# Second layers of tiles 1 and 2 as one 2x2 block problem of seven products

## The chip, the cores and the metric

One Trainium2 chip, one core. The metric is device time in microseconds. TensorE (PE) does the matmuls, VectorE (DVE), ScalarE (ACT) and GpSimd (POOL) the elementwise work, SyncE (SP) issues every DMA of the kernel from one queue.

## The reference

Causal attention over 4 batches, 12 heads, 448 positions and head size 64, then a two-layer network on its output:

```
scores = scale * q @ k^T, masked above the diagonal; attn = softmax(scores); o = attn @ v
x = o with its heads side by side                  # 1792 tokens x 768
h = x @ w_in                                        # 1792 x 2048
g = where(h > 0, h, exp(min(h, 0)) - 1)
out = g @ w_out                                     # 1792 x 768, float32
```

The weights w_in (768 x 2048) and w_out (2048 x 768) come as 64-bit floats; q, k and v as 32-bit floats.

## The kernel before

The 448 positions are cut into four chunks of 112. A *tile* (g = 0 to 3 in the code, tiles 1 to 4 here) is one chunk of all four batches: 448 token columns. Everything is kept transposed, so that a tile of x is 6 blocks of 128 rows by 448 columns, a tile of the hidden layer 16 such blocks, a tile of the output 6.

Attention works on pairs of heads (6 pairs p, 4 batches b, so 24 units a tile). For each unit TensorE makes scores, VectorE adds the mask and finds the largest (L326), ScalarE takes the exponential with its sum (L330), one of three engines scales (L564 to L570), TensorE transposes (L539), ScalarE or VectorE copies the transposes (L543, L544), TensorE multiplies by v into the accumulator `av` (L518). Tile g needs g + 1 chunks of k and v. In tiles 3 and 4 the scores are made from q and k split into a high and a low part (`parts`, L429), three matmuls each.

A product of the network is accurate to float32 by splitting both factors into a high and a low part in a short format and adding three matmuls (`three`, L679: high by high, high by low, low by high). Only the first 8 of 16 row blocks of tile 1's first layer use one plain float32 matmul (L703). `hi_lo` (L647) makes the split: a copy on ScalarE (or VectorE), a subtraction on VectorE (or GpSimd).

A weight piece is read as 64-bit words, converted to float32 by five steps (L620 on VectorE, L624 on ScalarE, L625 on VectorE, L628 on ScalarE, L631 on GpSimd) and stored to DRAM (`kin`, `kout`) for the tiles that follow. This is `weights` (L599). Pieces of w_in are 768 elements wide per partition (16 pieces), pieces of w_out 512 (24 pieces: 6 row blocks e, 4 groups x of 4 hidden blocks).

Tiles 1 and 2 go through the network one after the other: first layer (`emit_h`, 16 x 6 blocks), then second layer (`emit_o`, 6 x 16 blocks). `emit_h` ends a hidden block with the activation on ScalarE (L710, L711) and VectorE (L712) and splits it at once into gh and gl (L715, L716). While tile 2 uses the weights, `mixed` (L661) also makes four sums or differences of quarter blocks of each layer's weights and stores them (`sin`, `sout`).

Tiles 3 and 4 are taken together, as a 2x2 block problem: the weight halves by output rows and by inner dimension, and the two tiles as two column blocks. A product scheme with seven block products in place of eight (GROUPS, L810: 1, 2, 6, 7, 4, 5, 3) needs sums of weights (`sin`, `sout`, read back by `raw_piece`), differences of activations (`halves`, L788) and sums of results (`results`, L814). `mixed_h` does the first layer so, `mixed_o` the second. Their x rows (`xs`) wait in SBUF from attention on.

Buffers are rings: `PLACES` (L273) gives their number. A `Ring` hands its places out in a fixed order; a `Heap` hands out the place that was released first. Rows of 448 columns share one pool of SBUF, eight PSUM banks are shared by `hp` (3), `p` (4) and `av` (1).

The order of work is written by a planner (`Plan`). Every step is listed with estimated costs, what it reads and writes and, for matmuls, a due time; due times go back from a step to those it needs. It starts, step by step, the work that can start first, of several the one due first, and where two engines could do a step, the first unless the other would end sooner. What it finds is the fixed order of instructions of each engine. `SPREAD` (L983) says where attention is listed among the network's blocks, in estimated microseconds of network matmuls: tile 2's attention from 0 to 125, tile 3's to 185, tile 4's to 240. Tile 1's first layer is 67 of these, its second 60, tile 2's layers 60 each. `plan.cap` bounds the due time of `mixed` to 8 (LATER) after the block it is listed with.

## Time and profile before

| what | value |
|---|---|
| median of 3 runs | 644.68 us (644.46 to 646.44) |
| the profiled execution | 645.02 us, span 643.2 us |
| TensorE matmul busy | 620.4 us, 96%, 4032 instructions |
| VectorE, ScalarE, GpSimd busy | 517.0, 441.4, 192.4 us |
| granted clock, mean | 0.995 |
| DMA | 124.25 MB, 193 GB/s over the span |

A busy share is an average over stages. Matmuls are pipelined and overlap, so their busy time is more than their number times the distance between two starts. In the lists by group the figures behind the bar are busy time, the mean duration in ns, and how long the engine stood idle just before, with what ended that.

### The profile page before, as it was taken

To read this page: it belongs to the slowest core of one execution; us is meant where nothing else is said; L and a number is where in the kernel's file an instruction comes from. 1 tells how busy PE (TensorE), PEld (TensorE's weight loads), DVE (VectorE), ACT (ScalarE), POOL (GpSimd) and SP (SyncE) were. 2 spreads that over 40 slices of the span, in tenths; PEclk is the share of its full clock that TensorE was granted. 3 is DMA by queue.
4 is the path that set the end of the run, shared out by engine and by line. 5 is a ranking of instruction groups with operands and counts; after the bars stand their busy time and mean duration, and the time that the engine had idled before them with its cause. 6 is when DMAs were issued, how large, how long until landed. Compare 5 with 4: busy or idle time off the path is not lost. (4 is left out here: it accounts for less than half of the span.)

```text
span 643.2 us, 11841 instructions
## 1 busy us (share of the span) xinstructions
PE 620.4 (96%) x4032; PEld 523.9 (81%) x4032; DVE 517.0 (80%) x1192; ACT 441.4 (69%) x1007; POOL 192.4 (30%) x166
## 2 busy tenths in 40 slices
PE   5799998999999999999999999999999999999997
PEld 4655586888886888888888887899999988999996
DVE  5875888898766997999787898998767899998611
ACT  6898888885766988878786768666544867463300
POOL 1352434334243445453332323210100462100000
PEclk9999997999999999999999999999999999999999
DMA  9998576779887577586748765576343233353121
GB/s 229 300 369 319 197 242 211 231 237 319 276 259 236 171 252 237 171 265 221 243 153 247 217 195 166 182 236 193 115 107 115 98 100 98 121 144 104 44 61 44
DMA packets 108124, 124.25 MB, mean 193 GB/s; under 512 B 39840, under 2 KB 87968, under 8 KB 108064
## 3 DMA queue, kind: packets, MB, share of 16 engines
q1 hardware_dynamic: 108064, 123.50, 61.8%
q8 instruction: 32, 0.52, 0.3%
q14 instruction: 28, 0.23, 0.1%
HBM read 92.80 MB, written 30.67 MB: 192 GB/s over the span
## 5 line engine op out<-in xcount | busy, mean ns | idle before, releaser
L653 DVE TENSOR_TENSOR whl<-w,whl 128x768 fp32r<-128x768 f32 (+1 forms) x114 | 108.1, 952 | 17.8 <-ACT whl L650 16.3
L330 ACT ACTIVATE a<-a,nm 112x112 f32<-112x112 f32 (+3 forms) x192 | 97.0, 519 | 34.6 <-DVE nm L326 34.5
L650 ACT ACTIVATE whl<-w 128x768 fp32r<-128x768 f32 (+1 forms) x90 | 69.3, 772 | 52.1 <-PE op L684 27.0
L326 DVE CUSTOM_DVE_ANT_0 a<-sc,mask 112x112 f32<-112x112 f32 (+3 forms) x192 | 74.7, 442 | 26.2 <-PE sc L488 12.1
L631 POOL TENSOR_TENSOR w<-w,w 128x512 int32<-128x512 int32 (+1 forms) x40 | 62.7, 1569 | 98.3 <-DVE w L625 70.8
L682 PE MATMUL op<-gh,whl 128*128 128x448 f32 x192 | 73.3, 382 | 1.5 <-ACT whl L650 1.4
L684 PE MATMUL op<-gh,whl 128*128 128x448 f32 x192 | 70.9, 369 | 1.3 <-DVE whl L653 1.2
L683 PE MATMUL op<-gl,whl 128*128 128x448 f32 x192 | 70.1, 365 | 0.0
L682 PE MATMUL hp<-ph,whl 128*128 128x448 f32 x168 | 61.9, 369 | 1.7 <-DVE u L777 1.7
L682 PE MATMUL op<-ph,whl 128*128 128x448 f32 x168 | 61.5, 366 | 0.0
L684 PE MATMUL op<-ph,whl 128*128 128x448 f32 x168 | 61.5, 366 | 0.0
L683 PE MATMUL op<-pl,whl 128*128 128x448 f32 x168 | 61.5, 366 | 0.0
L683 PE MATMUL hp<-pl,whl 128*128 128x448 f32 x168 | 61.5, 366 | 0.0
L684 PE MATMUL hp<-ph,whl 128*128 128x448 f32 x168 | 61.4, 366 | 0.0
L682 PE MATMUL hp<-xh,whl 128*128 128x448 f32 x144 | 57.1, 396 | 3.0 <-ACT whl L650 3.0
L684 PE MATMUL hp<-xh,whl 128*128 128x448 f32 x144 | 53.9, 374 | 0.2 <-DVE whl L653 0.2
L683 PE MATMUL hp<-xl,whl 128*128 128x448 f32 x144 | 53.6, 372 | 0.0
L518 PEld LDWEIGHTS av<-at,v 112*64 112x64 f32 x864 | 41.6, 137 | 12.0 <-issue 7.3
L518 PE MATMUL av<-at,v 112*64 112x112 f32 x864 | 49.4, 263 | 0.0
L539 PE MATMUL tr<-ident,a 112*112 112x112 f32 x432 | 48.9, 263 | 0.0
L658 POOL TENSOR_TENSOR w<-w 128x384 f32<-128x384 f32 (+1 forms) x29 | 27.1, 933 | 63.2 <-DVE w L658 29.4
L539 PEld LDWEIGHTS tr<-ident,a 112*112 112x112 f32 x432 | 41.5, 133 | 5.4 <-issue 0.4
(121 smaller groups left out, 1392.4 us busy)
## 6 DMA issues: line engine op xcount, KB each, us to landing
w<-in_w_in SPq DMA_DIRECT2D x16, 768.0 KB, 6.8
w<-in_w_out SPq DMA_DIRECT2D x24, 512.0 KB, 5.6
w<-kin SPq DMA_DIRECT2D x28, 384.0 KB, 4.2
k<-in_qk SPq DMA_DIRECT2D x30, 224.0 KB, 4.3
kin<-w SPq DMA_DIRECT2D x16, 384.0 KB, 3.0
kout<-w SPq DMA_DIRECT2D x24, 256.0 KB, 4.5
sin<-w SPq DMA_DIRECT2D x16, 384.0 KB, 3.3
w<-kout SPq DMA_DIRECT2D x24, 256.0 KB, 4.1
```

The costliest lines, as they stand in the source:

```text
L326: plan.add(dve(n, lambda: nc.vector.tensor_tensor_reduce(out=a()[:, c], in0=sc()[:, c], in1=mask[:, S - n:], op0=ALU.add, op1=ALU.min, sca ...
L330: plan.add(act(n, lambda: nc.scalar.activation(a()[:, c], a()[:, c], AF.Exp, bias=nm()[:, x:x + 1], scale=-1.0, accum_out=su()[:, x:x + 1] ...
L518: nc.tensor.matmul(av()[half_of(half), chunk(o["b"])], o["v"]()[:, half, i], at()[:, chunk(x)], start=i == 0, stop=i == g,)
L539: nc.tensor.transpose(tr()[:, chunk(x)], o["a"][half]()[:, chunk(i)], ident)
L631: plan.add(pool(size, lambda: nc.gpsimd.tensor_tensor(out=wf().bitcast(I32), in0=wf().bitcast(I32), in1=low().bitcast(I32), op=ALU.add)), ...
L650: act(n, lambda: nc.scalar.activation(h(), x(), AF.Copy)),
L653: sub = lambda eng: lambda: eng.tensor_tensor(out=l(), in0=x(), in1=f32(h()), op=ALU.subtract)
L658: two = lambda eng: lambda: eng.tensor_tensor(out=out(), in0=x(), in1=y(), op=op)
L682: nc.tensor.matmul(acc(), wh(k), xh(), start=first, stop=False, skip_group_check=more)
L683: nc.tensor.matmul(acc(), wh(k), xl(), start=False, stop=False, skip_group_check=more)
L684: nc.tensor.matmul(acc(), wl(k), xh(), start=False, stop=last, skip_group_check=more)
```

## The change

Tile 1's first layer is followed directly by tile 2's first layer. The 32 activated hidden blocks stay in SBUF as whole rows `G`; they are split later, product by product. The second layers of tiles 1 and 2 are then done together by `mixed_o(0)`, the same seven products as for tiles 3 and 4, with three accumulators from `hp`. Each of its 28 weight pieces is read back from DRAM and split.

For that, all of w_out is converted before: `pair_o` is listed twelve times between 62 and 122 on the scale of SPREAD, each time two pieces, and makes their sums into the buffer of the second piece's words. The sums of w_in are made by `pair_i`, eight times between 130 and 215, which reads two pieces again. Attention is listed at 0 to 64 (tile 2), 64 to 122 (tile 3) and 122 to 215 (tile 4). Tile 1's first layer is 67 on that scale, tile 2's 60, the seven products 104.

The x rows of tiles 3 and 4 are stored to `xdram` and read back when `mixed_h` begins its first two groups. Rows that lived in two rings (`x`, `g`) come from one heap of 53 places, and `w` and `w6` are heaps; `k` has three places where it had five, and for tile 2 a k place holds two batches. The split q and k of tile 3 lie in rows of the heap instead of `w6`. The planner's estimate of a DMA is 60 plus 0.3 for each byte of a row, at most 390 GB/s, where it was 260. Of kout only the parts that a product reads are stored. `convert`, `fetch` and `in_two` are the parts of `weights`, taken apart.

```diff
     PLACES = dict(
-        q=2, k=5, v=5, a=8, at=5, x=18, g=2 * FT, m=2, ob=2, w6=8, w=5, nm=4, su=4, rr=4, hp=3, p=4, av=1, row=SPARE,
+        q=2, k=3, v=5, a=8, at=5, m=2, ob=2, row=53, w6=8, w=5, nm=4, su=4, rr=4, hp=3, p=4, av=1, bank=0,
     )
-    ROWS = ("q", "k", "a", "at", "x", "g", "m", "ob", "row")
+    ROWS = ("q", "k", "a", "at", "m", "ob", "row")
...
+    xdram = dram.tile([2, NP, P, S], F32, name="xdram")
+    xkept = {}
...
     def split_x(g, p, av):
+        if g >= 2:
+            x = new("ob", [P, S], name="xs")
+            take(x, av)
+            k = xkept[g - 2, p] = Buf(None, lambda: xdram[g - 2, p])
+            dma(224, P, lambda: nc.sync.dma_start(out=k(), in_=x()), [x], [k])
+            return
         if g == 0:
-            x = xf[p] = new("g", [P, S], name="xf")
-            plan.add([
-                act(S, lambda: nc.scalar.activation(x(), av(), AF.Copy)),
-                dve(S, lambda: nc.vector.tensor_copy(x(), av())),
-            ], [av], [x])
-        if g >= 2:
-            x = xs[g, p] = new("x", [P, S], name="xs")
...
-            return
-        xh = new("x", [P, S], F32R, "xh")
-        xl = new("x", [P, S], F32R, "xl")
+            x = xf[p] = row("xf")
+            take(x, av)
+        xh, xl = row("xh", F32R), row("xl", F32R)
         plan.add(act(S, lambda: nc.scalar.activation(xh(), av(), AF.Copy)), [av], [xh])
         plan.add(
             dve(S, lambda: nc.vector.tensor_tensor(out=xl(), in0=av(), in1=f32(xh()), op=ALU.subtract)), [av, xh], [xl]
         )
         xt[g, p] = xh, xl
...
+        done(q0, k0)
...
+    def parts(g, x, n):
+
+        if g == SPLIT:
+            th, tl = new("row", [P, S], F32R, "kh"), new("row", [P, S], F32R, "kl")
+            hi, lo = (lambda: th()[:, :n]), (lambda: tl()[:, :n])
+            get = lambda d, i, c: (th, tl)[i]()[d, c]
+            h = th, tl
...
+        for b in range(0, B, 2) if g == 1 else ():
+            k, t = new("k", [P, S]), new("v", [CP, 2, 2, 2, D], name="v2")
+            src = qk[b:b + 2, 2 * p:2 * p + 2, :, 1, :n].rearrange("b h d c -> (h d) b c")
+            dma(n, 2 * P, lambda k=k, src=src: nc.sync.dma_start(
+                out=k().rearrange("p (b c) -> p b c", b=2), in_=src
+            ), [], [k])
+            for i in range(2):
+                dma(112, 2 * CP, lambda t=t, i=i, b=b: nc.sync.dma_start(out=t()[:, i], in_=v[b + i, p, :, :, :2]), [], [(t, i)])
+                ks.append((None, [k], lambda d, x, c, k=k, i=i: k()[d, i * n + c.start:i * n + c.stop]))
+                vs.append((t, lambda half, x, t=t, i=i: t()[:, i, half, x]))
...
+    def convert(key):
+        r, w = words.pop(key), new("w", [P, KT, P])
+        n = KT if key[0] == "i" else 4
...
+        if key[0] == "i":
+            done(r)
+            home, src = kin[key[1]], wf
         else:
-            by = (lambda t: t) if key[0] == "i" else lambda t: t.rearrange("p (h k) c -> p h k c", h=2)
...
+            h = key[1] // HALF_E
+            home = kout[key[1]].rearrange("p (h f) c -> p h f c", h=2)[:, h:, 2 * key[2]:2 * key[2] + 2]
+            src = lambda: wf().rearrange("p (h f) c -> p h f c", h=2)[:, h:]
+        k = kept[key] = Buf(None, lambda: home)
+        dma(n * 64, P, lambda: nc.sync.dma_start(out=home, in_=src()), [w], [k])
+        return w if key[0] == "i" else (w, r)
+
+    def fetch(f):
+        w, k = new("w", [P, KT, P]), kept["i", f]
+        dma(KT * 64, P, lambda: nc.sync.dma_start(out=w(), in_=k()), [k], [w])
+        return w
+
+    def in_two(w, n):
+        t = new("w6", [P, 2, KT, P], F32R, "whl")
+        hi_lo(lambda: t()[:, 0, :n], lambda: t()[:, 1, :n], lambda: w()[:, :n], n * P, (t, 0), (t, 1), w)
+        done(w)
+        return t, (lambda k: t()[:, 0, k]), (lambda k: t()[:, 1, k])
 
...
+        if layer == 1:
+            add(b(1), b(0), b(1), n, ALU.add, [(wb, 0)], [(wb, 1)])
+            add(b(0), a(0), b(0), n, ALU.subtract, [(wa, 0)], [(wb, 0)])
+            add(a(0), b(1), a(0), n, ALU.subtract, [(wb, 1)], [(wa, 0)])
+            add(a(1), a(1), a(0), n, ALU.subtract, [(wa, 0)], [(wa, 1)])
+            for i, w in enumerate((wa, wb)):
+                dma(2 * h * 64, 2 * P, lambda i=i, w=w: nc.sync.dma_start(
+                    out=sin[r][:, :, i], in_=w().rearrange("p (h k) c -> p h (k c)", h=2)
+                ), [w], [(k, i)])
+            return
+        m = lambda i: lambda: f32(into().rearrange("p k c w -> p (k c w)"))[:, i * n:i * n + n].rearrange("p (k c) -> p k c", k=h)
+        add(m(3), b(0), b(1), n, ALU.add, [wb], [(into, 3)])
+        add(m(1), a(0), b(0), n, ALU.subtract, [(wa, 0), (wb, 0)], [(into, 1)])
+        add(m(0), m(3), a(0), n, ALU.subtract, [(wa, 0), (into, 3)], [(into, 0)])
+        add(m(2), a(1), m(0), n, ALU.subtract, [(wa, 1), (into, 0)], [(into, 2)])
+        dma(4 * h * 64, 4 * P, lambda: nc.sync.dma_start(
+            out=sout[x, :, :, :, r].rearrange("p h i c -> p (h i) c"),
+            in_=f32(into().rearrange("p k c w -> p (k c w)"))[:, :4 * n].rearrange("p (m c) -> p m c", m=4),
+        ), [into], [k])
...
     def emit_h(g, f, k, due):
         if k == 0:
...
+            if g == 0:
+                for n in range(0 if f == 0 else f + EARLY, min(f + EARLY + 1, FT)):
+                    load64(("i", n))
+                w = convert(("i", f))
+            else:
+                w = fetch(f)
+            st["w"] = (w,) if g == 0 and f < PLAIN else in_two(w, KT)
...
+        done(w[0])
+        o = G[0, f // HALF_F, g, f % HALF_F] = row("G")
+        elu(o, hp)
...
+    def load_pair(n):
+        x, e = divmod(n, HALF_E)
+        for d in (e, e + HALF_E):
+            load64(("o", d, x))
+
+    def pair_o(n, due):
+
+        for y in range(0 if n == 0 else n + EARLY_O, min(n + EARLY_O + 1, NX * HALF_E)):
+            load_pair(y)
+        x, e = divmod(n, HALF_E)
+        plan.cap = due + LATER
+        (wa, ra), (wb, rb) = [convert(("o", d, x)) for d in (e, e + HALF_E)]
+        done(ra)
+        mixed(2, e, x, wa, wb, rb)
+        done(wa, wb, rb)
+        plan.cap = 1e9
+
+    def pair_i(r, due):
+
+        plan.cap = due + LATER
+        two = [fetch(f) for f in (r, r + HALF_F)]
+        mixed(1, r, None, *two)
+        done(*two)
+        plan.cap = 1e9
...
+        bs = {}
...
         def begin(g):
+            for a in range(2):
+                for k in range(HALF_K):
+                    if g < 2:
+                        b = bs[a, g, k] = row("xs")
+                        src = xkept[g, a * HALF_K + k]
+                        dma(224, P, lambda b=b, src=src: nc.sync.dma_start(out=b(), in_=src()), [src], [b])
...
+    def mixed_o(pair):
         keep, st = {}, {}
+        bank = "bank" if pair else "hp"
...
+            if pair and i not in (1, 5):
                 banks.done(acc)
...
+    EARLY, EARLY_O = 4, 1
     FIRST, EACH, SLOW = 4.0, 3.0, 1.3
-    SPREAD = (0.0, 125.0, 185.0, 240.0)
+    SPREAD = ((0.0, 64.0), (64.0, 122.0), (122.0, 215.0))
+    PAIRS_O, PAIRS_I = (62.0, 122.0), (130.0, 215.0)
...
     for p in range(NP):
         first_pair(p, FIRST + EACH * p)
+    for g in range(1, NG):
+        spread(SPREAD[g - 1], list(attention(g)))
+    last = len(side)
+    side[-1] = (*side[-1][:2], lambda due, fn=side[-1][2]: (fn(due), after_attention()))
+    spread(PAIRS_O, [(1e-9, lambda due, n=n: pair_o(n, due)) for n in range(NX * HALF_E)])
+    spread(PAIRS_I, [(1e-9, lambda due, r=r: pair_i(r, due)) for r in range(HALF_F)])
+    side.sort(key=lambda x: x[0])
...
+    def run(items, slow=1.0):
         nonlocal t, moved
-        for c, fn, early in items:
...
+        for c, fn in items:
+            while side and side[0][0] <= moved:
+                _, ca, fa = side.pop(0)
                 fa(t)
...
+    run(layers(0), SLOW)
+    run(layers(1))
+    run(mixed_o(0))
+    assert not side
     ring("hp").lend(banks)
-    ring("w").lend(ring("ws"))
-    ring("w6").lend(ring("w6s"))
-    run([(c, fn, False) for c, fn in mixed_h()])
-    run([(c, fn, False) for c, fn in mixed_o()])
+    run(mixed_h())
+    run(mixed_o(1))
     t += 1.0
     with tc.manual_schedule():
         plan.run()
```

## Rows read from the trace of the kernel before

**Rows 1.** Windows by stage: us, busy us of each engine (instructions), clock, DMA share, GB/s

```profile
...
35.00:127.30 92.30, 89.29 (x465) 61.23 (x464) 73.34 (x177) 79.65 (x181) 37.71 (x26) 0.96 0.76 257
127.30:200.00 72.70, 71.30 (x443) 61.26 (x443) 56.00 (x131) 48.84 (x111) 27.12 (x21) 1.00 0.84 262
200.00:311.50 111.50, 110.83 (x891) 93.26 (x891) 100.72 (x259) 93.93 (x243) 50.02 (x45) 1.00 0.73 228
311.50:430.40 118.90, 117.74 (x998) 99.80 (x997) 103.28 (x253) 88.31 (x205) 36.95 (x37) 1.00 0.65 200
...
```

**Rows 2.** Waits of TensorE: total us, times, longest us

```profile
...
PE hp L682 <- ACT whl L650: 3.0, 1, 3.0
...
```

**Rows 3.** Windows of four stretches in which an engine or the queue is full

```profile
...
35.00:60.00 25.00, 25.00 (x117) 13.62 (x116) 15.15 (x49) 22.93 (x55) 10.05 (x8) 1.00 1.04 382
140.00:180.00 40.00, 40.00 (x268) 34.58 (x267) 31.21 (x83) 28.49 (x69) 15.09 (x12) 1.00 0.94 293
220.00:240.00 20.00, 19.74 (x161) 16.80 (x161) 19.89 (x48) 17.64 (x46) 9.69 (x9) 1.00 0.74 237
430.40:501.00 70.60, 70.60 (x347) 64.99 (x346) 55.55 (x82) 40.17 (x69) 4.35 (x4) 1.00 0.45 136
...
```

**Rows 4.** Windows of 3 us behind the longest wait

```profile
...
102.00:105.00 3.00, 3.00 (x8) 2.51 (x8) 3.00 (x4) 1.93 (x4) 2.22 (x1) 0.50 0.90 287
105.00:108.00 3.00, 3.00 (x10) 2.70 (x9) 3.00 (x10) 2.33 (x7) 0.21 (x1) 0.55 0.63 233
...
```

**Rows 5.** TensorE's groups by form in 35 to 127.3 us: busy us, mean ns

```profile
...
L494 PE MATMUL sc<-k,q 64*112 64x224 f32 x58 | 7.5, 371 | 0.0
L539 PE MATMUL tr<-ident,a 112*112 112x112 f32 x56 | 6.8, 264 | 0.0
L518 PE MATMUL av<-at,v 112*64 112x112 f32 x96 | 5.9, 265 | 0.0
...
```

**Rows 6.** VectorE's groups by form, whole run

```profile
...
L653 DVE TENSOR_TENSOR whl<-w,whl 128x768 fp32r<-128x768 f32 x72 | 72.6, 1011 | 9.5 <-ACT whl L650 8.7
L653 DVE TENSOR_TENSOR whl<-w,whl 128x512 fp32r<-128x512 f32 x42 | 35.6, 851 | 8.3 <-ACT whl L650 7.7
...
L716 DVE TENSOR_TENSOR gl<-hp,gh 128x448 fp32r<-128x448 f32 x32 | 19.7, 617 | 5.2 <-ACT gh L715 5.2
...
L620 DVE TENSOR_SCALAR w<-w 128x512 f32<-128x512 f32 x24 | 12.9, 536 | 0.0
...
L625 DVE TENSOR_SCALAR w<-w 128x512 uint32<-128x512 uint32 x24 | 10.2, 424 | 2.5 <-ACT w L624 2.5
...
```

**Rows 7.** ScalarE's groups by form, whole run

```profile
...
L650 ACT ACTIVATE whl<-w 128x768 fp32r<-128x768 f32 x61 | 51.3, 842 | 46.4 <-PE op L684 26.0 <-PE hp L684 16.0 <-DMA w<-kin 2.2
...
L715 ACT ACTIVATE gh<-hp 128x448 fp32r<-128x448 f32 x32 | 17.1, 536 | 3.3 <-DVE hp L712 3.1
L628 ACT ACTIVATE w<-w 128x512 int32<-128x512 uint32 x24 | 16.1, 670 | 0.0
...
L624 ACT ACTIVATE w<-w 128x512 f32<-128x512 f32 x24 | 15.1, 628 | 8.0 <-DVE w L620 4.6 <-issue 3.2
...
```

**Rows 8.** Windows of line 658 alone (columns: us, VectorE, GpSimd, clock, DMA)

```profile
...
200.00:311.50 111.50, 11.50 (x19) 17.47 (x17) 1.00 0.73 228
311.50:430.40 118.90, 18.30 (x39) 10.90 (x13) 1.00 0.65 200
...
```

**Rows 9.** GpSimd's group of the wide-word adds by form, whole run

```profile
...
L631 POOL TENSOR_TENSOR w<-w,w 128x512 int32<-128x512 int32 x24 | 32.1, 1339 | 54.8 <-DVE w L625 50.8 <-DMA w<-in_w_out 4.0
...
```

**Rows 10.** Line 620: count, durations in ns min/median/max, first and last start

```profile
...
L620 DVE TENSOR_SCALAR w<-w x40: 409/426/2241, 28.9 to 195.5; 128x512 f32<-128x512 f32 x24, 128x768 f32<-128x768 f32 x16
...
```

**Rows 11.** VectorE's groups by line in 200 to 311.5 us

```profile
...
L653 DVE TENSOR_TENSOR whl<-w,whl 128x768 fp32r<-128x768 f32 (+1 forms) x12 | 12.0, 1003 | 2.8 <-ACT whl L650 2.6
L564 DVE TENSOR_SCALAR a<-a,rr 112x336 f32<-112x336 f32 x26 | 12.0, 511 | 0.2
L432 DVE TENSOR_TENSOR khl<-k,khl 128x336 fp32r<-128x336 f32 (+1 forms) x18 | 11.9, 688 | 0.0
...
```

More of the change, by code (lines that the diff above doesn't have):

```diff
@@ L84, with __init__ @@
 class Heap(Ring):
[L87 to L88 removed]
+    def __init__(self, places=0, long=False):
+        super().__init__(places, long=long)
     def new(self, make):
@@ L285, in ring @@
         if tag not in rings:
-            heap = tag in ("row", "bank", "ws", "w6s")
-            rings[tag] = Heap() if heap else Ring(PLACES[tag], tag != "p", tag in ("w", "w6"))
+            long = tag[0] == "w"
+            rings[tag] = Heap(PLACES[tag], long) if tag in HEAPS else Ring(PLACES[tag], tag != "p", long)
         return rings[tag]
@@ L384, in split_x @@
         xt[g, p] = xh, xl
-    first = [(new("g", [P, S], name="q0"), new("g", [P, S], name="k0")) for _ in range(NP)]
+    first = [(new("row", [P, S], name="q0"), new("row", [P, S], name="k0")) for _ in range(NP)]
     def first_pair(p, due):
@@ L453, in loads @@
             ), [], [t])
-            if split:
-                kk = new("w6", [P, 2, S], F32R, "khl")
-                parts(kk, k, n)
-                k = kk
-            ks.append(k)
-            vs.append(t)
-        return dict(q=qq if split else q, k=ks, v=vs, a={}, at={})
+            ks.append(parts(g, k, n) if split else whole(k))
+            vs.append((t, lambda half, x, t=t: t()[:, half, x]))
+        return dict(q=qq, k=ks, v=vs, a={}, at={})
     def attention(g):
@@ L659, in add, with mixed @@
         plan.add([dve(n, two(nc.vector), port=True), pool(n, two(nc.gpsimd))], reads, writes)
-    def mixed(layer, r, x, wa, wb):
+    def mixed(layer, r, x, wa, wb, into=None):
         h = HALF_K if layer == 1 else 2
```

283 lines of the change are left out of this document (91 added, 192 removed).

## The prediction

> **What bounds the kernel now.** I read the windows by stage first [rows 1]. They cut the run where the work of TensorE changes: 35 to 127.3 us is the first layer of tile 1, 127.3 to 200 its second layer, 200 to 311.5 the first layer of tile 2, 311.5 to 430.4 its second layer. In all four the matmul row is busy for nearly the whole stretch. Its longest wait there comes next [rows 2]: 3.0 us, once, in the first stretch. So matmuls set the time, and the reader should look at how close the others are: in the third stretch VectorE and ScalarE together are busy 194.7 of 223 us, 87%, with GpSimd at 50.0 us beside them; in the first they are at 153.0 of 184.6, 83%; the DMA engines stand at 0.73 to 0.84. The kernel is matmul bound with little cover. The pace of a matmul is not its mean duration, because they overlap: where nothing else runs, 347 of them took 70.6 us, 0.2035 us each [rows 3].
>
> **What a wait costs.** The 3.0 us wait of [rows 2] lies in the first stretch; the granted clock behind it was 0.50 and 0.55 of full speed, 1.2 GHz instead of 2.4, from 102 to 108 us [rows 4]. Counting what was not granted in those 6 us of work (1.5 and 1.35 us), a wait of 3 us cost nearly 6 us.
>
> **The change, part by part.**
>
> *Matmuls removed.* The second layers of tiles 1 and 2 are 2 x 96 blocks of three matmuls, 576. Seven products of 4 x 3 x 2 blocks are 168 blocks, 504. The difference is 72 x 0.2035 = 14.65 us, all on the engine that sets the end. That is the gross gain.
>
> *Stretch A, tile 1's first layer.* It now holds all of tile 2's attention, where it held 58 of 96 score matmuls, 56 of 96 transposes and 96 of 192 value matmuls [rows 5]. Per piece these took 0.13, 0.12 and 0.06 us, so 4.9 + 4.8 + 5.9 = 15.6 us of TensorE come in: 92.3 + 15.6 = 108 us. The two vector engines do 153.0 us there now [rows 1]. They lose the gh and gl steps, 16 x (0.536 + 0.617) = 18 us [rows 6, 7], and about 14 us on second-layer weights converted ahead; they gain some 43 us of attention (half of a tile's softmax, scaling and copies, judged by the softmax counts). That makes 164 of 216 us, 76%; counting every instruction of the stage anew gives 183, 85%. Below the 87% at which the third stretch keeps matmuls running, so I charge nothing beyond the wait of [rows 2], which I leave where it is (bounds: 6 us gained if it goes, 12 lost if two more like it come).
>
> *Stretch B, tile 2's first layer.* Matmuls are those of 200 to 311.5 us less 16 stray ones of tile 1's second layer (3.3 us), and less the first scores of tile 4 net of the first layer's last block, which ends behind it (about 0.9): 107.3 us. Vector work changes as follows. Out: mixed sums of the first layer, 32 of the 36 adds that L658 had there (10.2 us VectorE, 15.5 GpSimd) [rows 8]; gh and gl, 16 x 0.536 on ScalarE (8.6) and 16 x 0.617 on VectorE (9.9) [rows 6, 7]; some 6 us of second-layer pieces. In: all 24 conversions of w_out, on VectorE 24 x (0.536 + 0.424) = 23.0, on ScalarE 24 x (0.628 + 0.670) = 31.2, on GpSimd 24 x 1.339 = 32.1 [rows 6, 7, 9]; their 48 mixed sums, about what L658 cost in the fourth stretch, 16 and 10 us [rows 8]. VectorE and ScalarE: 194.7 - 10.2 - 9.9 - 8.6 - 6 + 23.0 + 31.2 + 16 = 230 us; GpSimd 50 - 15.5 + 32.1 + 10 = 77. Two engines have 214.6 us while the matmuls take 107.3. So B no longer fits under its matmuls. The fullest row is 220 to 240 us, 37.5 of 40 us, 94% [rows 3]; at that share 230 us need 122.5. The planner may place a conversion up to 8 us after the weight row it is listed with, and most of w_out is needed only in the next stretch, so I let 8 us run over: 114.5, a loss of 7.2 us. Bounds: 0 if GpSimd takes the surplus, 24 by the rival below.
>
> *Stretch C, the second layer of both tiles.* 118.9 us plus 216 matmuls x 0.2035 = 44.0 makes 163 us. Vector work there is 191.6 us [rows 1]; out go 24 narrow weight splits, 24 x (0.628 + 0.851) = 35 (VectorE's from [rows 6], ScalarE's that of a copy as wide [rows 7]), mixed sums 16, output copies 6; in come 28 wide weight splits x (0.842 + 1.011) = 52, 56 activation splits x (0.536 + 0.617) = 65, 32 differences and 21 sums at 0.617 = 33 [rows 6, 7], the moved mixed sums 10, and 15 from B: 310 of 326 us, 95%. GpSimd, busy 37 us, can take some of the splits; 30 us there bring it to 91%. I charge 0 for the work itself. The three accumulators are new as a limit: the next product may write the first only when it is drained, four blocks (2.4 us) after its last matmul, and a drain of 0.62 us can stand behind a 1 us split. Six such handovers: 0 to 6 us, I take 1, nearest to the third and fourth stretches, where three accumulators already cost next to nothing (TensorE busy 110.8 of 111.5 and 117.7 of 118.9). Behind a waiting first matmul stands everything else on TensorE, as it issues in order.
>
> *Places.* Fifty-three row places are one heap. Near the end of B 30 first-layer rows and 12 of x leave 11, one pair's ten split q and k rows: the next pair's splits wait until the last scores of the one before have read theirs, about 0.5 + 0.6 us each time, and what queues behind them on ScalarE and VectorE with them. TensorE has first-layer blocks to do meanwhile; 0, with 0 and 6 us (five pairs) as bounds. A k load that finds three places for five waits likewise.
>
> *x through DRAM, moved DMAs.* Twelve stores and twelve loads of 224 KB are added, sixteen more loads of w_in, 28 wide loads in place of 24; 12 sout stores go instead of 24, kout stores shrink. Sum: 14 MB more. The stores go out while attention still runs and nothing waits for them soon. The loads sit before the paired first layer, whose stretch used 0.45 of the DMA engines [rows 3], and are issued in order on SyncE with the weight loads; queued behind one that waits they would come late, and the first matmuls of that layer with them. Cover: six rows are asked for before the products of C end. I take 0, bounds 0 and 9 (one landing with its split, doubled by the clock as above). The two paired layers themselves are unchanged.
>
> *Sum.* The profiled execution took 645.02 us. 645.0 - 14.65 + 7.2 + 1 = 638.6; the median of the runs shown, 644.68, is 0.3 lower, so 638.5.
>
> **A rule weighed.** A VectorE instruction that had a minimum of 409 ns and a median of 426 took up to 2241 ns [rows 10]: it stood behind GpSimd's adds. The Trainium skill, SBUF — State Buffer, "Who interferes with whom", says that VectorE with two SBUF inputs or in a two-port mode and GpSimd share one port pair as an exclusive lock, one blocking the other fully. By that rule GpSimd's 77 us in B would not be extra capacity, and B would be the rival below; the trace agrees that blocking happens.
>
> **Rivals.**
> 1. *Matmuls stay the bound* in B too: GpSimd and a shift of work into C absorb the surplus. For it: VectorE was busy 19.89 of 20 us in one row with TensorE still at 19.74 [rows 3]. Against: 107% of two engines. Time 645.0 - 14.65 = 630.3.
> 2. *Slower: VectorE and GpSimd take turns in B.* GpSimd's 50.0 us and VectorE's two-input and scaling work there now (L653 12.0, L564 12.0, L432 11.9 [rows 11], L658 11.5 [rows 8], in sum 47.4) make 97.4 of 111.5 us: it just fits. The conversions add 23.0 + 32.1: 152.5. Giving GpSimd's 44 us of optional work back to VectorE, at half the time, leaves 130.5 against 107.3, and with nothing run over: +23.2, with the handovers' 1 us. Time 645.0 - 14.65 + 24.2 = 654.6. It decides once B passes 107.3 + 14.65 = 122 us. Against: the durations of VectorE already hold blocked time, and work may run over.
> 3. *The DMA queue in B.* w_out 12.6 MB, w_in again 6.3, stores of kout 4.7, sout 6.3 and x 1.4, attention loads 9.6: 40.9 MB (sizes from the shapes). In the second layer of tile 1 293 GB/s at a share of 0.94 is 312 at full share [rows 3]: 131 us. With the half of its stores that can wait put off, 6.2 MB, 111. Between them 121: +14, no change, 645. For w_in's long rows the share of 1.04 gave 382 GB/s, which speaks for less.
>
> **How the numbers follow.** Forecast 638.5: 0.40 (its own range 633 to 642.7). Rival 1: 0.20. Rival 3: 0.12. Rival 2: 0.28. What a measurement can tell from no change is about 0.3%, 1.9 us: faster is under 642.7, slower over 646.6. So faster 0.60, same 0.12, slower 0.28. The range reaches to rivals 1 and 2: 629 to 656.
>
> **What would show it.** 504 matmuls in tile 1 and 2's second layer at 0.2035 us, and 72 fewer in all: the gross gain. B's length between tile 2's first and last first-layer matmul: 107 means rival 1, 115 the forecast, over 122 rivals 2 or 3; there a row of TensorE waits ended by w_out's conversions or weight splits, with VectorE and ScalarE near 94%, is mine; VectorE instructions of 0.43 us stretched beyond 2 us by the dozen is rival 2; weight splits that wait for DMA at a share near 1 is rival 3. A clock below 1.0 for more than one stretch of 6 us in A or B would mean that waits of 3 us and longer have multiplied, and the forecast is too low. A wait of the paired first layer's first matmul on x would show the DRAM step uncovered.

## The result, and the profile after

The changed kernel takes 652.48 us (median; 651.38 to 654.09) against 644.75 for the kernel before on the same chip: a ratio of 1.0116, 95% interval 1.0088 to 1.0145. It is slower. The forecast was 638.5, so its direction was wrong; the time lies inside its range and 2 us below the slower rival's 654.6.

The profiled execution took 651.38 us with a span of 649.6. A profile is of one execution, and those read below lie up to 3.6 us from the median of their run (639.4 us for the run called on, profiled at 643.0), so a few microseconds between stretches of two runs say little. The page's first part (busy us, share of the span, instructions):

```profile
PE 615.2 (95%) x3960; PEld 514.6 (79%) x3960; DVE 554.6 (85%) x1202; ACT 459.0 (71%) x1035; POOL 229.4 (35%) x177
```

TensorE has 72 matmuls less, VectorE and GpSimd are busier. These are the stretches B (tile 2's first layer) and C (the second layers of both tiles) of the changed kernel; columns as in [rows 1].

```profile
141.54:270.10 128.56, 116.88 (x867) 95.67 (x868) 121.98 (x290) 115.62 (x284) 65.79 (x59) 0.95 0.93 302
270.10:436.90 166.80, 161.60 (x1202) 138.68 (x1202) 155.93 (x297) 124.64 (x267) 69.73 (x49) 1.00 0.77 242
```

Against the forecast, stretch by stretch (us; 649.6 - 634.3 = 15.3 us to be explained). The prediction's stretches add up to 634.3, which is 2.4 less than the span that its own sum gives (643.2 - 14.65 + 8.2 = 636.7); it does not say where these lie.

| stretch | forecast | measured |
|---|---|---|
| head, up to the first matmul of the plain rows | 35.0 | 38.0 |
| A, tile 1's first layer | 108.0 | 103.5 |
| B, tile 2's first layer | 114.5 | 128.6 |
| C, second layers of tiles 1 and 2 | 164.0 | 166.8 |
| paired first layer | 105.5 | 105.6 |
| paired second layer | 107.3 | 107.1 |

B alone misses by 14.1 us; the rest nearly cancels. (The head's 3.0 us go with a granted clock of 0.87 there, where the kernel before had 1.00.) In B TensorE is no longer busy throughout: 11.7 us of it are idle, and its clock is 0.95, where the third stage of [rows 1] had 110.8 of 111.5 us at 1.00. The waits of TensorE in B of the changed kernel (total us, times, longest us):

```profile
PE hp L701 <- DVE whl L660: 4.4, 3, 3.7
PE tr L553 <- ACT a L581: 2.1, 1, 2.1
PE av L532 <- ACT at L557: 1.5, 1, 1.5
PE sc L504 <- DVE kl L444: 1.2, 2, 1.0
...
```

Every one ends with a result of VectorE or ScalarE, the longest with a weight split. It lies at 260 to 264 us; the windows of 3 us around it in the changed kernel (us, busy us of PE, PEld, DVE, ACT, POOL, clock, DMA share, GB/s):

```profile
258.00:261.00 3.00, 2.11 (x15) 1.32 (x11) 3.00 (x6) 0.85 (x1) 0.41 (x1) 1.00 0.94 271
261.00:264.00 3.00, 0.20 (x1) 0.21 (x2) 3.00 (x6) 2.77 (x7) 1.36 (x2) 0.92 1.02 330
264.00:267.00 3.00, 3.00 (x12) 2.18 (x14) 2.39 (x8) 2.35 (x6) 2.29 (x3) 0.51 1.10 288
267.00:270.00 3.00, 3.00 (x20) 2.47 (x17) 2.92 (x9) 2.88 (x5) 3.00 (x5) 1.00 1.08 370
```

The reader is to see the order: VectorE is busy for all six microseconds, TensorE runs dry, and once it starts again its clock is at 1.2 GHz (0.51) for one window, as in [rows 4]. The wait cost 3.7 us and the clock behind it 1.5 more. Over B a clock of 0.95 means 0.05 x 128.6 = 6.4 us not granted (an estimate, as 0.95 is rounded), so B is some 110.5 us of matmuls, 11.7 of waits and 6.4 of clock. The clock fell three times in B: behind the wait of 2.1 us above (0.51 from 144 to 147 us), behind three waits of together 1.8 us from 206 to 210 us (0.50 and 0.55 from 210 to 216 us), and here.

Why VectorE was late can be seen in single instructions. In the timeline of B of the changed kernel (start and duration in us; in brackets how long the engine had been idle, and what ended that; rows between are left out):

```profile
162.75 1.30 POOL L629 TENSOR_TENSOR w<-w,w 128x512 int32<-128x512 int32 x1 [0.99 <-DVE w L623]
162.99 1.42 DVE L444 TENSOR_TENSOR kl<-k,kh 128x336 fp32r<-128x336 f32 x1 [0.32 <-ACT kh L443]
...
173.64 0.50 DVE L444 TENSOR_TENSOR kl<-k,kh 128x336 fp32r<-128x336 f32 x1
173.81 1.50 POOL L629 TENSOR_TENSOR w<-w,w 128x512 int32<-128x512 int32 x1 [3.54 <-DVE w L623]
174.06 1.67 DVE L658 CAST whl<-w 128x768 fp32r<-128x768 f32 x1
...
207.61 1.61 POOL L629 TENSOR_TENSOR w<-w,w 128x512 int32<-128x512 int32 x1 [0.70 <-DVE w L623]
207.99 1.60 DVE L444 TENSOR_TENSOR kl<-k,kh 128x336 fp32r<-128x336 f32 x1
...
209.64 0.62 PE L504 MATMUL sc<-kl,kh 64*112 64x336 f32 x2 [0.96 <-DVE kl L444]
...
261.80 1.13 POOL L444 TENSOR_TENSOR khl<-k,khl 128x448 fp32r<-128x448 f32 x1 [3.39 <-ACT khl L443]
...
261.98 1.76 DVE L660 TENSOR_TENSOR whl<-w,whl 128x768 fp32r<-128x768 f32 x1
...
```

The same subtraction takes 0.50 us when it starts ahead of a GpSimd add and 1.42 us when it starts inside one: it ends 0.36 us after the add does. The cast at 174.06 is held in the same way. At 207.99 the whole chain can be seen: GpSimd adds, the subtraction that starts inside the add takes 1.60 us, TensorE waits 0.96 us for its result, and the clock is at 0.50 behind that. The weight split that ended the longest wait is the last row: 1.76 us instead of some 0.95. So about 0.8 of the 3.7 us were GpSimd's; for the rest VectorE was at other work.

### The profile page after: what moved, and what is told of

The parts are those of the page before. It is cut to its first block, busy times and chain, and to the rows that moved or that the text cites. A ratio compares the mean times of both kernels' runs of the same rounds, so it can differ in the third digit from the quotient of the medians.

```text
span 649.6 us, 11763 instructions
## 1 busy us (share of the span) xinstructions
PE 615.2 (95%) x3960; PEld 514.6 (79%) x3960; DVE 554.6 (85%) x1202; ACT 459.0 (71%) x1035; POOL 229.4 (35%) x177
## 4 chain that ended last, share of the span: by engine, by line
PE 48%; DVE 17%; DMA 15%; ACT 11%; issue 5%; SPq 2%; POOL 2%; ACTq 0%; DVEq 0%; POOLq 0%
PE op L699 7%; PE op L700 7%; PE op L701 7%; PE hp L701 4%; PE hp L721 4%; PE hp L699 4%; PE hp L700 4%; ACT a L336 4%; DMA w<-in_w_out 3%; DVE whl L660 3%; DMA k<-in_qk 3%; PE sc L504 2%; PE tr L553 2%; DMA xs<-xdram 2%; DMA v<-in_v 2%
## 5 line engine op out<-in xcount | busy, mean ns | idle before, releaser
L699 PE MATMUL op<-ph,whl 128*128 128x448 f32 x336 | 125.7, 374 | 3.8 <-DVE s L785 1.8
L700 PE MATMUL op<-pl,whl 128*128 128x448 f32 x336 | 123.2, 367 | 1.3 <-DVE pl L660 1.3
L701 PE MATMUL op<-ph,whl 128*128 128x448 f32 x336 | 123.1, 366 | 0.0
L657 ACT ACTIVATE whl<-w 128x768 fp32r<-128x768 f32 x86 | 72.5, 843 | 59.8 <-PE op L701 30.3
L660 DVE TENSOR_TENSOR whl<-w,whl 128x768 fp32r<-128x768 f32 x97 | 101.2, 1044 | 9.1 <-ACT whl L657 8.1
L629 POOL TENSOR_TENSOR w<-w,w 128x512 int32<-128x512 int32 (+1 forms) x40 | 65.9, 1650 | 81.8 <-DVE w L623 36.0
L699 PEld LDWEIGHTS op<-ph,whl 128*128 128x128 f32 x336 | 63.2, 188 | 13.6 <-issue 3.2
L700 PEld LDWEIGHTS op<-pl,whl 128*128 128x128 f32 x336 | 63.2, 188 | 6.8 <-DVE pl L660 1.8
L701 PEld LDWEIGHTS op<-ph,whl 128*128 128x128 f32 x336 | 63.1, 188 | 5.3
L660 POOL TENSOR_TENSOR pl<-G,ph 128x448 fp32r<-128x448 f32 x25 | 35.6, 1436 | 53.7 <-DVE ph L658 25.0
L553 PE MATMUL tr<-ident,a 112*112 112x112 f32 x432 | 51.1, 267 | 3.0 <-ACT a L581 2.1
```

Of the source, the lines that this page charges most:

```text
L553: nc.tensor.transpose(tr()[:, chunk(x)], o["a"][half]()[:, chunk(i)], ident)
L629: plan.add(pool(size, lambda: nc.gpsimd.tensor_tensor(out=wf().bitcast(I32), in0=wf().bitcast(I32), in1=low().bitcast(I32), op=ALU.add)), ...
L657: act(n, lambda: nc.scalar.activation(h(), x(), AF.Copy)),
L660: sub = lambda eng: lambda: eng.tensor_tensor(out=l(), in0=x(), in1=f32(h()), op=ALU.subtract)
L699: nc.tensor.matmul(acc(), wh(k), xh(), start=first, stop=False, skip_group_check=more)
L700: nc.tensor.matmul(acc(), wh(k), xl(), start=False, stop=False, skip_group_check=more)
```

## The experiments

All are the changed kernel with one edit unless said otherwise. The theories are: V, VectorE and ScalarE together have too much work for B (the forecast's own step, mis-sized); P, VectorE and GpSimd take turns, so GpSimd's work lengthens VectorE's (rival 2); and D, the DMA queue is full (rival 3). Rows are the windows of B, and of C where a second row stands, with the columns of [rows 1].

**Conversion steps left out, for the w_out pieces alone** (`off` is true for them).

```
e1:  L622 Prelu (ScalarE), L623 shift (VectorE), L626 low part (ScalarE), L629 add (GpSimd): left out
e2:  L629 add (GpSimd): left out
e3:  L622, L626 left out; L623 -> min, L629 -> float add w + w, same shapes
```

> The changed kernel with four of the five conversion steps of w_out left out (only the clamp to float32 range stays, so the second layers' weights are wrong); every DMA and the order of all else are as they were. In the stretch of tile 2's first layer (B, 126 us where its matmuls need 107) this takes about 31 us from ScalarE, 10 from VectorE and 32 from GpSimd. Theory V (ScalarE and VectorE are full in B): B falls to 108 to 112 and the time from 652.5 to 634 to 639. Theory D (the DMA queue is full in B): the bytes are the same, B stays over 120 and the time over 647. Theory P (VectorE and GpSimd take turns): like V.

Measured: 642.33 us, ratio 0.9971 (0.9946 to 0.9997). B in this run:

```profile
145.70:259.90 114.20, 110.21 (x869) 91.86 (x868) 99.44 (x267) 94.99 (x241) 35.85 (x39) 0.99 1.03 333
```

10.2 us of the 652.5 and 14.4 of B go with the conversions. That is less than V and P had promised, and against D. What is left, 114.2 us, has the DMA engines full (1.03 at 333 GB/s): below that the queue is likely to be next.

> The changed kernel without the last conversion step of w_out alone, the add on GpSimd (24 x 1.34 us; the weights then lack their low bits); DMAs and the order of all else as they were. Theory V: ScalarE and VectorE keep their work, B stays at 122 to 126, 649 to 653. Theory P: VectorE no longer waits for those 32 us, its instructions of 0.43 us are no longer stretched to 2, B falls to about 112, 637 to 642. Theory D: no change, 651 to 653.

Measured: 645.25 us, ratio 1.0005 (0.9988 to 1.0022). B:

```profile
142.61:262.70 120.09, 113.51 (x867) 94.27 (x868) 105.00 (x286) 114.59 (x280) 37.49 (x39) 0.96 1.00 322
```

An instruction that only GpSimd runs was taken away (28.3 us of it in B), and VectorE, with nearly the same instructions (286 for 290), is busy 17 us less. That is P, and the time falls by 7.2 of e1's 10.2 us. The size lies between the theories: P alone had B at 112 us. A conversion is also one step shorter in this run; what that is worth by itself it does not show.

> As the changed kernel, but for the 24 pieces of w_out both conversion steps on ScalarE are left out (24 x (0.628 + 0.670) = 31 us of ScalarE), VectorE's shift is a minimum of the same shape and GpSimd's add is a float add of the piece with itself, same shape: the w_out values are wrong, everything else and the order are kept. Theory P (VectorE and GpSimd take turns in tile 2's first layer, ScalarE has slack): VectorE stays at about 122 us busy and GpSimd at about 66, so the stretch stays at 126 to 129 us and the time at 650 to 653. Theory V (VectorE and ScalarE together are simply too full, 237 of 257 us): 31 us less of work in two engines, 15 us each at 94%: the stretch falls to 114 to 116 us and the time to about 640, as when four of the five conversion steps went.

Measured: 647.01 us, ratio 1.0046 (1.0023 to 1.0069). B:

```profile
145.22:263.50 118.28, 110.87 (x870) 91.11 (x869) 112.72 (x280) 93.08 (x240) 59.45 (x55) 1.00 0.97 316
```

B shrinks by 10.3 us and the time by 5.5, though GpSimd does nearly what it did. P alone promised nothing here, V twice as much of the total. So neither theory seems to stand alone. But the run is no clean test of ScalarE's part: VectorE's busy time fell by 9.3 us too, with 10 instructions fewer in the window and a replaced GpSimd add that is shorter (1260 ns for 1410).

**The DMA queue.**

```
e4:  twelve w_out loads (512 KB each) left out; the piece is made from its twin's words
e5:  for to in (sout, again): nc.sync.dma_start(out=to[x, ...], ...)      # stored twice
```

> The changed kernel in which the second piece of each pair of w_out is converted from the words of the first, so that twelve loads of 512 KB (6.3 MB) are left out; the work of ScalarE, VectorE and GpSimd is the same (the weights of half the output rows are wrong). The planner's order shifts a little. Theory D: B moved 37.9 MB at 301 GB/s, 6.3 MB less is up to 21 us, so B falls to about 110 and the time to 638 to 643. Theory V and P: 649 to 653.

> The changed kernel with each of the twelve stores of w_out's mixed sums (512 KB) issued twice, the second to memory that nothing reads: 6.3 MB more, most of it in B, with no other work. Theory D: B grows by 12 to 17 us, 664 to 670. Theory V and P: B has 7% of its DMA time free and stores can wait, 652 to 655.

Measured: e4 654.07 us (ratio 1.0153, 1.0107 to 1.0199), e5 659.49 (1.0236, 1.0212 to 1.0259). B of e4 took 129.07 us at a DMA share of 0.84, B of e5 134.23 at 1.01. Six megabytes less gain nothing, six more cost 7 us, between the 652 to 655 of V and P and the 664 to 670 of D: the queue was not the limit of the changed kernel, but is close behind it. (e4 also lets the second conversion of a pair wait for the words of the first.)

**Less GpSimd.** Two edits: the optional two-input work stays on VectorE until the paired layers begin (n1, the result is the same), and the last conversion step of all 40 pieces becomes one VectorE instruction (o1; a step of ScalarE changes with it, so that each weight is cut to 24 bits and not rounded).

```
n1:  -plan.add([dve(n, two(nc.vector), port=True), pool(n, two(nc.gpsimd))], reads, writes)
     +plan.add(ways([dve(...), pool(...)]), reads, writes)     # ways: the first alone before mixed_h
o1:  -tensor_scalar(w, w, 3, op0=logical_shift_left)           # VectorE
     -gpsimd.tensor_tensor(out=w, in0=w, in1=low, op=add)
     +scalar_tensor_tensor(out=w, in0=w, scalar=3, in1=low, op0=logical_shift_left, op1=bitwise_or)
on:  both
```

> As the changed kernel, but until the paired layers begin GpSimd may take none of the optional two-input work (sums of weights, second parts of q, k, weights and rows): all of it stays on VectorE, which does it in about half the time. Results unchanged; the planner orders the work anew. In tile 2's first layer that is about 33 us of GpSimd (9.8 + 2.4 + 2.0 + 6.8 + 5.0 + 4.1 + 2.3 + 2.3) turned into about 17 us of VectorE. Theory V (sum of VectorE and ScalarE): 17 us more in two engines, 9 us each: the stretch 136 to 139 us, the time about 660. Theory P (turns on one port): 33 us of turns become 17, the busy time of VectorE stays near 122 (17 more of work, 17 less of blocking): the stretch 118 to 128 us, the time 644 to 652.

> As the changed kernel, but the last conversion step is taken from GpSimd for all 40 pieces: VectorE's shift becomes a shift and an OR with the low part in one instruction, and ScalarE's step truncates the low part instead of rounding it (so each weight is cut to 24 bits, not rounded). GpSimd loses 40 x 1.34 us, VectorE gains 40 x about 0.2. Theory P: in tile 2's first layer VectorE's busy time falls by 17 (the blocking that went when that step was left out) less 5, to about 110, and the stretch to 118 to 122 us, the time to 643 to 647. Theory V: 5 us more of VectorE, nothing less of the two engines: the stretch 129 to 131, the time 652 to 655. The DMA queue (share 1.03 with 114 us, 333 GB/s) keeps the stretch from falling below about 114.

> o1_or_step and n1_less_gpsimd together, with the changed kernel's own spread (64, 122, 215; PAIRS_O to 122). Results unchanged but for the cut of the weights to 24 bits. If GpSimd's turns are the whole of what tile 2's first layer lost, the time is 633 to 638, as with the later spread (634.5). If the crowding of that stretch is a cost of its own, VectorE and ScalarE have about 225 us there and the stretch takes about 120: 639 to 645.

Measured: n1 650.66 us (1.0093, 1.0061 to 1.0125), o1 645.71 (1.0026, 0.9995 to 1.0057; it was profiled at 651.1, too far off for its windows to be read), on 639.44 (0.9929, 0.9901 to 0.9956). n1's time does not differ from the changed kernel's beyond the two intervals; it is its B that counts:

```profile
145.08:269.30 124.22, 114.39 (x869) 94.72 (x869) 118.51 (x307) 116.67 (x289) 33.62 (x27) 0.96 0.96 305
```

B and C of on:

```profile
138.63:260.40 121.77, 112.78 (x881) 93.11 (x880) 112.85 (x319) 116.38 (x289) 5.71 (x10) 0.99 0.98 315
260.40:428.40 168.00, 162.06 (x1202) 140.14 (x1201) 161.10 (x339) 129.16 (x276) 10.90 (x10) 0.99 0.78 245
```

In on VectorE took over all that GpSimd did in B except the scaling (some 17 us of sums and second parts, half of GpSimd's 33, and 5 for the longer OR), and is busy 9.1 us *less*: 121.98 to 112.85. So some 31 us of VectorE's busy time were waiting for 60 us of GpSimd (an estimate, as the planner also ordered the work anew). V had n1 at 136 to 139 us in B; it was 124. Yet with GpSimd all but idle B of on still takes 121.8 us, 9.0 of them with TensorE idle, and the time is the 639 to 645 that was expected if the crowding of B has a cost of its own: V holds beside P. The forms of VectorE show what P took, in B of the changed kernel (busy us, mean ns):

```profile
L332 DVE CUSTOM_DVE_ANT_0 a<-sc,mask 112x336 f32<-112x336 f32 x45 | 20.1, 499 | 0.2 <-PE sc L504 0.2
...
L623 DVE TENSOR_SCALAR w<-w 128x512 uint32<-128x512 uint32 x19 | 9.9, 526 | 2.3 <-ACT w L622 2.1
L665 DVE TENSOR_TENSOR w<-w,w 128x256 f32<-128x256 f32 x17 | 9.6, 562 | 0.5
L618 DVE TENSOR_SCALAR w<-w 128x512 f32<-128x512 f32 x19 | 9.5, 507 | 0.0
L444 DVE TENSOR_TENSOR kl<-k,kh 128x336 fp32r<-128x336 f32 x12 | 9.5, 794 | 0.3 <-ACT kh L443 0.3
L658 DVE CAST whl<-w 128x768 fp32r<-128x768 f32 x3 | 4.6, 1529 | 0.0
```

and in B of on, where the lines have moved by one or two:

```profile
L334 DVE CUSTOM_DVE_ANT_0 a<-sc,mask 112x336 f32<-112x336 f32 x48 | 21.4, 500 | 0.8 <-PE sc L506 0.8
...
L446 DVE TENSOR_TENSOR kl<-k,kh 128x336 fp32r<-128x336 f32 x19 | 9.4, 500 | 0.0
L664 DVE TENSOR_TENSOR w<-w,w 128x256 f32<-128x256 f32 x20 | 8.4, 419 | 0.2
L620 DVE TENSOR_SCALAR w<-w 128x512 f32<-128x512 f32 x19 | 7.9, 420 | 1.6 <-DMA kout<-w 0.9 <-DVE at L560 0.5
L657 DVE CAST whl<-w 128x768 fp32r<-128x768 f32 x3 | 1.7, 554 | 0.3 <-DMA w<-kin 0.3
```

The subtraction goes from 794 to 500 ns, the sum from 562 to 419, the cast from 1529 to 554: nineteen of the first in 9.4 us, where twelve took 9.5. The step that reads TensorE's scores from PSUM and the mask from SBUF is in the first row of each list: 499 ns in the mean beside a busy GpSimd, 500 without. Of its 45 instructions 34 overlap one of GpSimd, and none is longer for it. So GpSimd holds up some instructions of VectorE and not others.

A count by instruction gives a like size. Take as the free length of a form the median of its instructions that overlap none of GpSimd, over the runs here. VectorE's 290 instructions in B of the changed kernel are then 24.5 us too long in sum, 31 of them by more than 0.1 us. The 286 of e2 are 9.3 us too long, the 259 of the third stage of the kernel before 9.4.

**Where the work sits.**

```
     SPREAD                                   PAIRS_O          PAIRS_I     EARLY
changed  ((0, 64), (64, 122), (122, 215))     (62, 122)        (130, 215)    4
h6       ((6, 64), (64, 122), (122, 215))     (62, 122)        (130, 215)    4
s1       ((0, 64), (64, 134), (134, 222))     (62, 132)        (135, 222)    2
s2       as s1, with o1;   s4: as s1, with on
s3       ((0, 56), (56, 130), (130, 222))     (62, 132)        (135, 222)    3, with o1
s5       as s3, with on
```

> As the changed kernel, but tile 2's attention is spread from 6 instead of 0 on, so that its loads come behind the last ones of the first attention; all results unchanged. If those loads hold the first attention up, the head is back from 38 to 40 us to 35 and the half clock in it goes: 648 to 650 in all, tile 2's first layer unchanged. If the head is long for its own queue order, it stays at 38 to 40 and the time at 651 to 654.

> As the changed kernel, but part of the work of tile 2's first layer may come later: SPREAD ((0, 64), (64, 134), (134, 222)) moves a sixth of tile 3's attention into the stretch of the second layers, PAIRS_O ends at 132 instead of 122, PAIRS_I (135, 222), and two w_in loads are issued ahead instead of four. Results unchanged. If the first layer of tile 2 is long because too much vector work is set beside its matmuls and the next stretch can take some, that stretch falls from 128.6 to 113 to 118 us, the second layers grow from 166.8 to 172 to 175, and the time falls to 644 to 648. If the vector engines are equally full in both (VectorE 122 of 129 and 156 of 167 us), the work only moves: 650 to 654.

> s1_spread_later and o1_or_step together: later spread, and the last conversion step of all pieces on VectorE as shift and OR in one. Results unchanged but for the cut of the weights to 24 bits. Theory P (GpSimd's turns lengthen VectorE's work) and the crowding add up: o1_or_step gave 6.8 us of 652.5, the later spread 4 to 8: 638 to 642, faster than the kernel before. If only one of the two matters, 644 to 648.

> As s2_spread_or, but tile 2's attention is done by 56 instead of 64, tile 3's by 130, and three w_in loads are ahead: 3 to 5 us of vector work go from tile 2's first layer into tile 1's, which had matmuls busy 46.7 of 47.4 us with VectorE at 43.9. 636 to 642 if that has room; if not, tile 1's first layer waits and the time is 642 to 648.

> As s2_spread_or, but until the paired layers begin GpSimd takes none of the optional two-input work either, so it has almost nothing left beside VectorE there: results as s2_spread_or. If the turns on the port are the cost, VectorE's instructions shrink to their undisturbed length (0.43 us for the 512-wide step that had a mean of 0.51) and the time is that of s2_spread_or or up to 4 us less, 636 to 641. If GpSimd's help counts as capacity (about 70 us of it in the second layers, 35 us of VectorE), VectorE overflows there and the time is 5 to 12 us longer than s2_spread_or.

> s4_spread_or_less_gpsimd with s3_earlier_spread_or's spread ((0, 56), (56, 130), (130, 222)), three w_in loads ahead. Tile 1's first layer then has VectorE and ScalarE about 4 us fuller, the stretches behind it as much emptier; it was 5.5 us faster with GpSimd at work. If VectorE in the second layers (169 of 174 us) sets that stretch, 630 to 634; if the matmuls already do (168 of 174), the same 632 to 637.

Measured:

| run | us | ratio | 95% interval |
|---|---|---|---|
| h6 | 660.45 | 1.0257 | 1.0219 to 1.0295 |
| s1 | 659.09 | 1.0232 | 1.0189 to 1.0275 |
| s2 | 648.42 | 1.0056 | 1.0033 to 1.0080 |
| s3 | 642.87 | 0.9996 | 0.9969 to 1.0023 |
| s4 | 634.52 | 0.9850 | 0.9802 to 0.9899 |
| s5 | 632.21 | 0.9820 | 0.9785 to 0.9856 |

h6 has its head back at 35.6 us and loses more behind it, so the head's 3 us are not worth buying back that way. h6 and s1 are slower, and s4 faster, than anything that was expected of them. s2 missed what was expected of it: with GpSimd's optional work still there, the OR and the later spread did not add up (648.4 for 638 to 642). s1 shortens B and overfills C, and is slower; the same spread with GpSimd out is faster than both kernels. B and C of s1:

```profile
143.49:253.30 109.81, 104.34 (x783) 86.81 (x784) 104.21 (x256) 103.12 (x253) 52.31 (x46) 1.00 0.95 304
253.30:445.10 191.80, 177.95 (x1286) 149.74 (x1286) 178.26 (x321) 143.61 (x310) 88.72 (x67) 0.95 0.75 238
```

and of s4:

```profile
138.26:243.10 104.84, 101.24 (x783) 85.26 (x783) 96.53 (x270) 101.88 (x253) 7.44 (x13) 1.00 0.99 325
243.10:417.50 174.40, 168.28 (x1285) 143.85 (x1285) 169.36 (x359) 138.12 (x299) 19.24 (x21) 1.00 0.82 258
```

GpSimd's 88.7 us in C fall to 19.2; VectorE, which took that work, falls from 178.3 to 169.4; TensorE's idle time falls from 13.9 to 6.1 us, its clock returns to 1.00, and C is 17.4 us shorter. I had held it possible that VectorE would overflow there; the opposite came.

**GpSimd's time by itself.** s4 with work that nobody waits for:

```
d1:  +idle_add: gpsimd.tensor_tensor(out=extra, in0=a[:, :256], in1=a[:, :256], op=add)   # 96 times
```

> s4_spread_or_less_gpsimd with work for GpSimd that nobody needs: behind the scaling of each attention row of tiles 3 and 4 GpSimd adds 256 columns of the row to themselves into a scrap tile, 96 times some 0.8 us = 77 us. Results and all needed work unchanged. If the turns on the port cost VectorE its time: leaving 32 us of GpSimd out took 17 us from VectorE, so 77 us should add some 40 us to VectorE's busy time in the two stretches (96.5 + 169.4 us in s4_spread_or_less_gpsimd), both are then full, and the time goes from 634.5 to 645 to 655. If GpSimd's work was slow only for those who waited for its results, nobody waits here, VectorE's busy time stays at 266 us and the time within 2 us of 634.5.

Measured: 648.62 us (1.0059, 1.0030 to 1.0088), 14.1 more than s4. GpSimd's group of it, in the two stretches:

```profile
L483 POOL TENSOR_TENSOR extra<-a 112x256 f32<-112x256 f32 x96 | 77.0, 802 | 75.2 <-DVE a L587 68.5 <-ACT a L590 1.1 <-DVE at L567 0.2
```

and B and C:

```profile
140.13:250.60 110.47, 102.91 (x785) 86.07 (x785) 103.19 (x272) 102.72 (x253) 35.59 (x54) 1.00 0.97 309
250.60:429.50 178.90, 173.36 (x1286) 147.41 (x1284) 171.66 (x356) 138.24 (x298) 60.90 (x68) 0.97 0.78 246
```

Direction as P has it: nobody needs the results, and B and C grow by 10.1 us. The size was wrong: VectorE's busy time rises by 9 us, not 40. One reason is in the adds themselves: they took 612 ns at least and 624 in the median, but 802 in the mean, so some 17 of their 77 us (96 x 0.178, an estimate) were GpSimd waiting in its turn. The longest, 2927 ns, lasts through four VectorE instructions of usual length. The rest of the profiled difference, which is 17.8 us where the medians differ by 14.1, is 1.8 us in the head and 5.7 us in the paired first layer, where TensorE waited 4.1 us for a copy of its accumulator; s5, without busywork, has that wait too (2.9 us), so I don't put it down to the port. The planner also ordered the work anew around the extra instructions, and an attention row `a` is not free for its next use until its add is done (one wait of TensorE, 0.7 us, ends with such an add). So not each of the 10 us is the port's for certain.

**The kernel before, with the same two edits.**

```
b1:  before.py with o1 and n1, its own order and blocks
```

> The kernel before with the two GpSimd edits alone (last conversion step on VectorE as shift and OR, no optional work on GpSimd until the paired layers), its order and block products unchanged. It was matmul bound (waits of 1 to 4 us in each stretch), so there is little to win: 641 to 645. Then the seven products are worth 644.5 - 634.5 = 7 to 11 us of their 14.65 once GpSimd is out. If GpSimd's turns cost the kernel before as much, it falls to 634 to 638, and the seven products are worth little.

Measured: 639.36 us (0.9929, 0.9904 to 0.9954): 5.1 us faster than it was. on, the changed kernel with the same edits, took 639.44 on the same chip. The gain has one place, tile 1's first layer:

```profile
35.20:121.07 85.87, 85.87 (x462) 58.66 (x463) 70.83 (x179) 78.22 (x173) 4.22 (x6) 1.00 0.83 277
```

It took 92.3 us at a clock of 0.96 before [rows 1]; its wait of 3.0 us and the half clock behind it are gone. GpSimd does less in the stages behind it as well (62.2 us in the whole run, where it did 192.4), but there TensorE had been busy nearly throughout, and they take nearly as long as they did. (A conversion is one step shorter here too, so the turns may not be the whole of the 5 us.) Freed of most of GpSimd's work the two kernels are equal, and the seven products win only when the work is spread anew: s5 is 7.2 us below b1. The kernel before was not spread anew, so how much of the 7.2 is the products' is not shown.

## Why the prediction was wrong, point by point

*The gross gain* was right: the page has 3960 matmuls of all kinds, 72 fewer, and C took 166.8 us where 177.5 would have stood with all blocks (118.9 of [rows 1] and 288 x 0.2035).

*Stretch A* was right to take no loss: 103.5 of 108 us, and with the head, 3 us longer, 141.5 of 143. The wait of [rows 2], left standing in the forecast, is gone from it.

*Stretch B* is the step that failed: "at that share 230 us need 122.5", then "I let 8 us run over: 114.5". The first half holds once GpSimd is out of the way: VectorE and ScalarE have 229.2 of 243.5 us in on, 94%, and 95% in n1 and s4. That on's 229.2 us are so near the 230 is luck: five of the 24 conversions were done in A, 11 us that I had counted in B, and on holds VectorE work that the sum gave to GpSimd. Two things were wrong.

Nothing ran over. The last GpSimd add of a w_out conversion starts at 249.5 us, 20 us ahead of the end of B. C had little room for more: VectorE alone was busy 155.9 of its 166.8 us, 93% (with ScalarE 84%, where I had put the two at 91 to 95%), and s1, which lists more work there, made C 25.0 us longer while B became 18.8 shorter. That the want of room is what kept the work in B is likely, not shown.

And GpSimd's work was counted as free capacity beside VectorE's. With it the two engines were busy 237.6 us instead of 229.2, though GpSimd did 22 us of their work: B went from 121.8 to 128.6. Eight and seven make the 14.1 us within 1, as near as two profiles can be compared. The bound of 24 us held.

*Rival 2* gave B 130.5 us and the time 654.6; measured 128.6 and 652.5. Its mechanism is what e2, n1, on and d1 show, its place is right, and its point of decision (B over 122) was passed. Its arithmetic was not, and the 2 us by which it missed are in part luck: it gave no part to ScalarE, though B is crowded without GpSimd too (on), and it added up all of GpSimd's time with VectorE's. The sign that it named, instructions of 0.43 us stretched beyond 2 us by the dozen, did not come: of 38 such in B (L618, L623) one took 2.1 us and two more over 1.2. The loss lies in many forms, a few tenths to 1.7 us at a time. The rule of the Trainium skill's page SBUF — State Buffer, "Who interferes with whom", is that VectorE with two SBUF inputs or in a two-port mode and GpSimd lock each other out of one port pair. The trace agrees with it: single instructions of VectorE are held until GpSimd is done, and the step that reads scores from PSUM is not. The runs do not bear the lock out as a sum over all work of the two engines: 70 us more of GpSimd in d1 took 9 us from VectorE.

*My reason against it*, that "the durations of VectorE already hold blocked time", was true of [rows 10], and misled. (Its 2241 ns belong to an instruction 768 wide, whose usual length is 0.55 us and not 0.43.) Those were the lengths beside the GpSimd work of the kernel before; B has more of it, and e2, with 28 us of it left out, has VectorE 17 us less busy. And the kernel before already paid for its own: b1 gains 5 us, all of it in tile 1's first layer.

*Rival 1* fell with B. *Rival 3* fell by e4; a DMA share of 1.03 in e1 makes it the likely next limit. (The DMA share of the four stages before was 0.65 to 0.84, not 0.73 to 0.84 as the prediction has it [rows 1].)

*The clock.* I priced one wait at double its length and added no new ones. In B the waits cost 11.7 us and the clock behind them 6.4.

*Handovers, places and x through DRAM.* The waits of TensorE in C of the changed kernel (total us, times, longest):

```profile
PE op L699 <- DVE s L785: 1.8, 1, 1.8
PE op L700 <- DVE pl L660: 1.3, 1, 1.3
PE op L699 <- DVE u L785: 1.3, 1, 1.3
PE op L699 <- DVE xs L781: 0.7, 1, 0.7
```

Three of them are handovers of an accumulator (the `xs` one of attention's), 3.8 us where I took 1 of 0 to 6. With the wait on a row split that is some 4 us more than forecast; the matmuls took 161.6 us for the 163 that I had, and so C missed by 2.8. No matmul waited for x.

## What to carry to other kernels

An engine that shares a path with another one is not spare capacity: before moving work beside it, find out which instructions of the other it can hold up, price that, and try the version in which it does nothing. When a stretch is over-full, work runs over only into a stretch that has room, so the neighbour's share belongs in the same sum. A reordering that saves on one engine may be worth nothing until the others' work is laid out for it: with most of GpSimd's work out of both kernels they were equal, and only the later spread put the changed one ahead.

## What was not expected of the hardware

Giving VectorE some 22 us more to do made it 9 us less busy (121.98 to 112.85 us in B), because GpSimd did 60 us less. One VectorE instruction that shifts and ORs in 0.69 us (mean of 19 in on) replaces a shift of 0.53 and a GpSimd add of 1.41. And a small move of where attention sits can cost as much as the change did: h6, a start 6 units later, was 8 us slower than the changed kernel, with the clock at 0.97 in both parts of A.
